# A mask and the norm's weights applied by column scalings on ScalarE in place of tensor operations on VectorE, with a new order of issue

## Chip, cores and metric

The kernel runs on one core of a Trainium2 chip. The core has five engines that run their own instruction streams and wait for each other by semaphores: TensorE (PE in the profile, PEld for its weight loads), VectorE (DVE), ScalarE (ACT), GpSimd (POOL) and SyncE (SP, which here only issues transfers). The metric is device microseconds of one launch. The kernel before took 1108.51 us, the median of three runs that lie between 1103.67 and 1111.27 us.

## What is computed

Two blocks follow each other. The first is a recurrence over 768 tokens for 4 batches of 8 heads with 40 channels each:

```
y[t]  = r[t] . state
Sa    = state . a[t]
state = state * w[t] - Sa (x) b[t] + v[t] (x) k[t]      # state is 40 x 40 per head
```

The second is a feed-forward block on the 3072 rows of 320 numbers that come out of the first:

```
x  = x / sqrt(mean(x*x) + 1e-6) * rms_g                 # rms_g: one weight per column
out = (silu(x @ w_gate) * (x @ w_val)) @ w_out          # 320 -> 1536 -> 320
```

All inputs are given as float64 or float32 and the products run in float32.

## The kernel before

The 768 tokens are cut into 24 chunks of C = 32 tokens; all 32 sequences (4 batches x 8 heads) of a chunk are worked on together. Each chunk has three stages:

- `front(c)` loads the chunk's tokens, turns them with TensorE, and builds the decayed keys and the products between tokens of the chunk, level by level (distances 1, 2, 4, 8, 16). Its result is a triangular matrix per sequence, in `LT`, which goes through DRAM (`sB`) into the layout `M`.
- `inverse(c)` inverts these triangles on VectorE: 31 steps, each a multiplication into `tmp` and a subtraction from `Yi` which depends on it and which the next step depends on. The result goes through DRAM (`sY`) back into `LT`.
- `main(c)` carries the state across the chunk and computes the outputs. Here the product `score` gives a 32 x 32 matrix per sequence in PSUM (`sc`). For each of the five levels a masked part of `sc` is written to `As` (192 instructions in all, lines 853 to 863), then five `level` products read `As`, and `y` gathers them. Afterwards `y` is turned (`turn4`), normalised into `x` by ScalarE, turned once more (`turn3`), and multiplied by the norm's weights `gcol` into `xg` (line 920), with the model's channels on the partitions.

Two chunks make a group. `feed(g)` runs the feed-forward block for a group: for each of 12 slices of the hidden width it makes two products of `xg` with a weight slice `wf` (gate and value), `Silu` of the gate on ScalarE into `sg`, the product of both on VectorE into `hT`, and the output product into `po`. For the first group the weights are also converted from float64 by integer operations on VectorE and ScalarE (`narrow`, tiles `wf`, `ex`, `o`), and kept in DRAM (`sW`).

PSUM is used as three pairs of banks (`ps0` to `ps2`) for everything but `po`. A product takes a pair and holds it until all that read it are issued. A pair is one tile; the framework that sets the semaphores also makes two engines that read the same bank wait for each other.

Nothing is scheduled while the kernel is built. Every operation is recorded as a piece (`Plan.add`), with what it depends on, and the pieces are then issued one by one in the order that the table `ORDER` gives, with the PSUM pair that the table `PAIRS` gives. A number in `ORDER` names the next piece, counted from the first one that is not issued yet, and a "-" issues a filler product of the identity (line 1000) which keeps TensorE active; there are 280 of them, all before the first output products. So the order of each engine's instructions is fixed by a table that the kernel only plays back, and each engine runs its own in that order.

All recorded operations of a kind have one line in the profile, that of the helper: 475 is every VectorE operation, 502 a copy on ScalarE, 498 an activation, 505 a scaling on ScalarE (`scale`), 518 a transfer, 521 a product, 524 a turn. So the profile is read by tiles.

Of the kernel before, what the change touches and what calls it, by code (L numbers as in the profile page):

```python
# [7 lines left out]
FP32 = mybir.dt.float32  # L8
# [8 lines left out]
P = 128  # L17
C = 32
LEVELS = (1, 2, 4, 8, 16)
CG = 2  # L20
WB = 5
S0, S1 = 15.0, 2.0
LEAD = 2
WARM = 230.0
# [21 lines left out]
36 33 2 26 42 1 31 0 25 343 37 29 107 38 24 36 26 34 262 2 13 1 35 40 0 190 24 339 13 14 - - - 40 17 44 15 41 43 55  # L46
42 8 60 47 175 72 48 45 84 185 59 68 186 585 54 58 - - - - - 49 93 586 53 179 69 71 599 81 176 57 597 50 67 178 609
70 188 80 622 51 92 16 623 65 610 52 56 177 633 64 66 - - - - - - - - - - - - 61 189 9 598 77 79 187 78 587 620 62 0
587 81 - - - - 72 75 179 82 62 90 595 384 194 588 87 11 633 89 589 74 395 620 197 590 380 88 73 195 391 - - - - 101
196 209 390 610 84 102 214 381 201 611 202 5 212 86 213 383 591 85 0 222 92 591 611 17 95 221 224 223 384 94 234 225  # L50
- - 197 233 237 93 391 245 246 592 328 393 198 598 645 612 0 641 598 15 612 592 - 338 205 206 380 642 599 209 0 207
612 200 0 337 612 186 598 6 326 613 2 599 641 34 176 200 216 217 23 600 389 215 33 201 355 95 202 177 96 214 - - - -
211 187 339 93 0 577 0 561 578 297 579 171 192 53 187 191 - - - 182 188 200 623 172 185 625 186 580 562 581 612 355
582 199 1065 197 583 611 183 198 624 184 0 152 1005 850 298 0 298 0 837 295 0 0 0 83 130 298 148 0 298 83 0 507 307
833 0 303 555 0 840 307 0 290 0 67 125 316 314 0 132 125 67 0 0 131 314 0 286 325 0 130 0 298 130 0 291 292 - - - -
- 287 0 293 0 304 0 316 305 301 0 0 283 0 296 0 311 0 322 281 0 286 0 295 280 0 292 - - - - - - - - - - - - - - - -
- 288 0 0 0 0 301 0 285 62 301 116 305 0 283 250 116 0 - - - - - - - - 293 0 258 112 296 0 110 300 256 0 308 307 245
293 292 0 0 304 0 288 0 301 - - - - - - 298 306 0 0 313 0 297 0 0 0 293 310 494 301 0 494 0 302 0 0 299 492 0 0 296
0 246 0 791 0 0 0 787 0 0 93 468 2 796 94 469 0 94 462 794 0 467 93 94 290 461 95 462 96 468 511 97 469 291 98 470
481 289 99 292 471 0 99 100 101 471 102 472 103 481 511 104 482 105 488 106 489 107 483 2 490 108 109 0 293 109 490  # L60
0 108 0 0 379 0 379 387 0 387 369 0 405 378 387 406 0 - - - - - - - - - - - - - - - - - - - - - - - - - - - - - - -
- - - - - - - - - - - - - - - - - - - - - - - - - - - - - - - - - - - - - - - - 44 0 367 377 0 415 0 42 0 414 383 43
412 0 383 410 0 383 40 373 0 0 0 0 0 0 36 0 377 - - - - - - - - - - - - - - - - - 44 0 377 35 44 0 414 0 0 82 0 32 -
43 0 373 0 90 0 229 407 38 88 0 40 78 226 42 38 41 47 48 0 43 226 42 50 45 48 396 0 50 396 43 0 396 0 0 379 395 380
0 395 380 0 401 0 394 0 378 242 400 44 0 400 47 0 145 45 377 242 0 145 391 377 0 216 1 145 391 42 635 398 429 626
146 0 397 39 145 426 634 398 146 147 631 43 623 44 621 45 632 46 148 47 622 - - - - 639 375 376 149 48 416 239 641
830 150 399 377 640 840 0 150 641 653 48 838 151 658 152 645 828 - - - - - - 642 153 670 154 646 155 682 49 656 50
156 669 657 51 157 666 158 667 52 159 643 668 - - - - - - - 53 389 160 161 678 162 1 651 652 - 647 2 702 655 3 654 0
594 610 611 609 625 595 636 109 608 110 596 373 - - - - - - - - - - - 605 590 374 111 345 783 607 626 782 383 112
627 620 622 385 793 113 623 606 375 382 114 792 621 - - - - - - - 617 384 115 376 346 116 377 619 117 635 634 118  # L70
618 378 119 - - - - - 160 633 120 379 121 163 380 161 122 381 123 162 124 164 386 - - - - - - - - - 629 125 387 126
127 128 388 129 630 130 640 631 389 638 131 390 - - - - - 167 641 132 391 133 639 134 392 168 135 393 - - - - - 165
136 394 137 138 430 139 166 571 431 581 643 140 - - - 171 721 644 580 141 642 142 570 143 174 645 144 173 145 178 -
- - 182 175 146 177 147 172 150 149 179 - - - 180 148 637 176 185 732 432 186 433 0 1065 584 283 - 39 1064 36 582 38
284 638 37 40 635 583 0 17 635 480 625 567 497 40 18 624 498 41 284 568 626 42 285 499 627 43 570 286 642 636 44 500
2 706 287 45 643 897 0 493 500 501 643 287 897 656 644 648 2 45 597 907 502 649 494 0 457 860 458 0 613 0 457 611
552 0 - 596 457 621 598 0 622 0 456 595 610 853 457 622 458 634 854 0 505 - - - 500 360 765 521 361 449 531 519 764
504 532 543 362 508 363 0 500 517 543 501 4 515 363 502 364 506 419 514 365 5 366 516 367 0 367 419 368 421 369 370
420 422 44 0 370 - 430 371 44 0 3 40 0 367 426 368 369 370 504 371 37 372 373 374 375 429 376 526 525 521 377 505
522 0 338 466 390 339 397 377 9 340 391 341 392 342 430 393 398 343 480 440 400 378 439 395 387 429 396 394 403 408  # L80
388 0 403 0 342 474 700 403 578 0 700 403 342 709 490 343 0 474 7 696 405 343 709 475 403 344 0 487 706 472 0 485
695 10 343 704 404 0 404 0 4 404 37 405 0 401 31 337 481 402 45 0 474 3 337 338 41 339 402 0 42 3 0 398 705 399 471
50 335 400 898 336 703 470 401 337 37 907 338 339 402 27 480 699 908 704 340 403 341 897 479 486 701 889 343 700 584
478 890 713 714 481 899 702 719 28 706 559 900 342 712 29 560 731 30 0 531 9 0 9 683 684 17 10 0 10 454 0 450 552 10
451 0 10 672 0 672 - - - - - - - - - - - - - - - - 662 25 0 27 670 26 0 682 680 24 695 539 677 676 678 704 661 37 -
- - - 3 36 675 662 296 4 681 434 691 663 679 692 703 672 5 0 0 428 1 680 683 42 682 666 43 687 681 667 20 40 686 21
677 695 2 22 292 0 675 705 287 0 675 287 688 0 671 0 669 665 269 7 17 410 8 682 29 411 412 30 667 413 414 0 8 665 0
675 8 681 672 9 674 0 9 672 - - - - - - - - - - 481 0 9 37 483 411 0 471 0 25 5 401 6 402 403 404 471 7 39 405 473 -
- - - - - - - - - - - 16 0 0 28 8 27 397 0 397 28 0 397 0 654 462 0 5 396 36 8 397 398 37 399 14 47 462 15 0 457 10
723 44 3 11 43 458 583 644 21 12 646 582 4 13 645 461 0 571 21 13 572 458 393 22 14 394 15 466 0 391 455 19 0 372 0  # L90
16 436 0 694 28 5 27 442 6 695 371 439 7 0 696 0 451 370 435 6 760 0 745 0 428 0 741 362 425 0 751 433 362 741 0 748
362 0 425 423 358 733 0 358 0 744 358 432 359 360 0 427 428 0 7 359 0 359 15 0 359 360 6 0 425 0 428 442 359 360 361
362 363 364 0 360 361 742 362 0 362 363 364 419 365 742 366 367 2 368 423 751 369 370 371 372 373 424 675 374 7 0
424 2 0 1154 672 0 1154 421 422 732 432 738 0 669 730 1002 732 670 420 995 731 439 742 685 985 421 0 993 421 687 735
422 686 743 4 1002 423 748 736 991 424 746 983 366 757 367 759 368 425 992 369 744 0 369 746 371 757 755 370 759 768
425 767 736 582 0 582 3 583 584 0 584 751 0 582 746 774 0 731 0 431 737 731 747 421 745 0 731 364 580 0 580 739 581
582 439 583 584 2 424 585 740 757 0 759 740 753 754 760 585 755 586 750 366 587 424 588 365 589 425 364 590 419 591
363 752 592 593 0 347 174 346 175 331 176 342 177 0 177 178 0 178 7 179 342 180 181 359 182 8 183 184 185 186 187
188 189 12 341 190 352 191 192 349 193 194 350 224 195 196 351 0 222 9 224 5 0 4 217 7 0 214 328 335 218 16 332 226
219 343 344 0 417 223 267 338 182 224 266 183 13 184 276 185 0 183 222 184 274 185 186 223 187 330 188 20 189 338 0  # L100
229 223 0 223 188 189 190 191 226 194 227 192 3 225 229 193 224 239 4 0 231 4 0 228 7 233 193 234 238 235 338 339
236 340 532 341 239 12 530 240 194 241 533 195 242 541 197 243 0 538 240 9 608 10 241 536 338 4 13 339 527 242 340
192 539 243 341 342 343 244 0 339 340 240 341 342 0 538 342 240 343 0 16 343 324 344 539 737 345 346 538 727 540 552
# [290 lines left out]
def kernel(  # L394
# [41 lines left out]
    N = 8  # L436
# [116 lines left out]
    for j, l in enumerate(LEVELS):  # L553
        nc.vector.tensor_scalar(iw[:, 2], iw[:, 0], j, None, ALU.logical_shift_right)
        nc.vector.tensor_scalar(msk[:, j], iw[:, 2], 1.0, None, ALU.is_equal)
# [477 lines left out]
```

## Time and profile before

| | before |
|---|---|
| median of three runs | 1108.51 us |
| profiled execution | 1109.57 us, of which 1107.8 us from first to last instruction |
| VectorE, in `As` | 192 instructions: 144 of 128x256 and 48 of 128x512, 83.2 us |
| VectorE, in `xg` | 24 instructions of 128x384, 13.5 us |
| ScalarE, all | 989 instructions |
| filler products | 560 matrix instructions, 72.9 us |

How to read it: "busy" is the time in which an engine executed an instruction, as a share of the span. TensorE's is taken from ends that are modelled, so busy is not the same as at its peak. In a line of instruction groups the form `out<-in` names the tiles written and read, then comes the shape as partitions x elements, the count, the total busy time, the mean of one in ns, and the idle time of the engine just before these instructions, with what ended it. In a table of stretches each engine's busy time in that stretch stands with its number of instructions, then PEclk, the clock granted to TensorE as a share of the full one, and the share of the transfer engines. In a list of waits the columns are total us, number of waits, and the longest.

### The profile page before, as it was taken

The page shows a single profiled execution, that of the slowest core. Times are in us where ns is not written, and L with a number is a line of the kernel's source. Part 1 is how long each engine was busy: PE and PEld are TensorE (multiplying, and loading weights), DVE is VectorE, ACT ScalarE, POOL GpSimd, SP SyncE. Part 2 cuts the span into 40 slices and gives each one's busy share as a digit, 9 for nine tenths or more (in the row PEclk, how much of TensorE's full clock was granted, in tenths as well). Part 3 has the DMA queues.
Part 4 walks back from the last instruction along what each step waited for, and adds up shares of the span by engine and source line. Part 5 has one row for each costly group of instructions (what it writes and reads, how often), then busy time and mean ns, then how long its engine had stood idle before and what let it go on. Part 6 is the DMA issues. An engine that isn't in the chain of part 4 may idle for free.

```text
span 1107.8 us, 53122 instructions
## 1 busy us (share of the span) xinstructions
PE 1043.1 (94%) x23152; PEld 862.2 (78%) x23152; DVE 906.1 (82%) x3065; ACT 453.9 (41%) x989; POOL 302.4 (27%) x534
## 2 busy tenths in 40 slices
PE   5698889989999999999999999999999999999998
PEld 5597777867878877877877887877878788888876
DVE  5999998899798889799789689988878889798421
ACT  4645554644235335325335335325325335332211
POOL 7621344022323422412422422422303412200000
PEclk9799999989999999999999999999979999999999
DMA  7635555675645645546535635635546536434242
GB/s 158 155 75 155 132 115 133 188 225 143 160 120 121 157 104 141 132 118 151 126 99 139 149 107 150 142 96 151 119 108 149 126 109 150 108 108 130 80 141 80
DMA packets 171177, 145.43 MB, mean 131 GB/s; under 512 B 123712, under 2 KB 142080, under 8 KB 170944
## 3 DMA queue, kind: packets, MB, share of 16 engines
q1 hardware_dynamic: 152576, 119.06, 39.7%
q0 software_dynamic: 16192, 22.64, 10.5%
q8 instruction: 182, 2.98, 1.2%
q10 hardware_dynamic: 2176, 0.33, 0.2%
q14 instruction: 51, 0.42, 0.1%
HBM read 125.83 MB, written 16.12 MB: 128 GB/s over the span
## 4 chain that ended last, share of the span: by engine, by line
PE 59%; DVE 26%; issue 4%; DMA 4%; ACT 4%; POOL 2%; SPq 1%; DVEq 0%; POOLq 0%; ACTq 0%
PE ps L521 40%; PE po L521 11%; PE ps L524 8%; DVE LT L475 4%; DVE tmp L475 3%; DVE Yi L475 3%; DVE K L475 2%; DVE As L475 2%; DVE ex L475 2%; DVE wf L475 2%; DVE y L475 1%; SPq L518 1%; DVE Ab L475 1%; ACT K L502 1%; DVE r L475 1%
## 5 line engine op out<-in xcount | busy, mean ns | idle before, releaser
L521 PE MATMUL ps<-xg,wf 128*128 128x256 f32 (+1 forms) x1728 | 357.6, 395 | 2.5 <-DVE xg L475 1.6
L521 PEld LDWEIGHTS ps<-xg,wf 128*128 128x128 f32 (+1 forms) x1728 | 263.1, 190 | 58.0 <-issue 15.2
L521 PE MATMUL po<-wf,hT 128*128 128x320 f32 x576 | 178.6, 444 | 2.7 <-DVE hT L475 1.3
L475 DVE TENSOR_TENSOR tmp<-Yi,M 128x60 f32<-128x60 f32 (+24 forms) x744 | 156.1, 210 | 19.2 <-DMA M<-sB 3.0
L475 DVE TENSOR_TENSOR Yi<-Yi,tmp 128x60 f32<-128x60 f32 (+24 forms) x744 | 155.4, 209 | 15.9
L498 ACT ACTIVATE sg<-ps 128x256 f32<-128x256 f32 x144 | 53.6, 382 | 239.9 <-PE ps L521 222.9
L518 POOL DMA_DIRECT2D VU<-in_v_dram x92 | 53.3, 586 | 354.0 <-PE ps L524 207.5
L521 PEld LDWEIGHTS po<-wf,hT 128*128 128x128 f32 x576 | 102.3, 190 | 38.8 <-issue 3.7
L475 DVE TENSOR_TENSOR hT<-ps,sg 128x256 f32<-128x256 f32 x144 | 59.3, 419 | 54.7 <-ACT sg L498 53.4
L521 PEld LDWEIGHTS ps<-Ab,K 40*64 40x64 f32 x4608 | 77.8, 139 | 30.5 <-issue 9.7
L475 DVE TENSOR_TENSOR K<-K,T 128x512 f32<-128x512 f32 (+1 forms) x192 | 93.5, 495 | 8.8 <-ACT K L502 3.0
L521 PE MATMUL ps<-Ab,K 40*64 40x56 f32 x4608 | 87.4, 226 | 11.2 <-DVE K L475 3.1
L502 ACT COPY K<-K 128x256 f32<-128x256 f32 (+1 forms) x168 | 71.3, 443 | 61.8 <-PE ps L521 38.5
L475 DVE TENSOR_TENSOR As<-ps,msi 128x256 f32<-128x256 f32 (+1 forms) x192 | 83.2, 481 | 13.1 <-PE ps L521 12.9
L502 ACT COPY KN<-ps 128x640 f32<-128x640 f32 x96 | 66.4, 692 | 54.8 <-PE ps L524 21.4
L521 PEld LDWEIGHTS ps<-As,KN 128*40 128x40 f32 x3072 | 67.2, 125 | 18.7 <-issue 10.7
L521 PE MATMUL ps<-As,KN 128*40 128x32 f32 x3072 | 74.5, 206 | 6.1 <-issue 3.4
L1000 PE MATMUL po<-ident 128*128 128x128 f32 x560 | 72.9, 284 | 5.3 <-ACT po L544 5.3
L518 POOL DMA_DIRECT2D kbn<-in_b_dram x92 | 53.8, 587 | 83.0 <-PE ps L521 72.3
L518 POOL DMA_DIRECT2D wn<-in_w_dram x92 | 51.5, 565 | 85.7 <-DVE tmp L475 32.5
L518 POOL DMA_DIRECT2D kbn<-in_k_dram x92 | 53.3, 583 | 75.0 <-PE ps L521 74.3
L1000 PEld LDWEIGHTS po<-ident 128*128 128x128 f32 x560 | 67.6, 197 | 6.7 <-POOL wan L514 5.2
(124 smaller groups left out, 1546.8 us busy)
## 6 DMA issues: line engine op xcount, KB each, us to landing
wf<-sW SPq DMA_DIRECT2D x144, 480.0 KB, 4.1
M<-sB SPq DMA_DIRECT2D x96, 128.0 KB, 3.7
rn<-in_r_dram SPq DMA_DIRECT2D x24, 160.0 KB, 4.3
sW<-ex SPq DMA_DIRECT2D x16, 240.0 KB, 3.0
out_dram<-o SPq DMA_DIRECT2D x48, 80.0 KB, 3.6
kbn<-in_b_dram POOLq DMA_DIRECT2D x92, 40.0 KB, 3.1
wan<-in_w_dram POOLq DMA_DIRECT2D x46, 80.0 KB, 4.2
wan<-in_a_dram POOLq DMA_DIRECT2D x46, 80.0 KB, 4.0
```

The costliest lines, as they stand in the source:

```text
L475: plan.add("DVE", time + more + each * size(o), 0.087, lambda at: fn(at(o), *m(at)), [o], aps(*args))
L498: scalar(o, [a], lambda at: nc.scalar.activation(at(o), at(a), f, **kw), aps(acc), 0.1 if f in (AF.Square, AF.Relu) else 0.0)
L502: scalar(o, [a], lambda at: nc.scalar.copy(at(o), at(a)), extra=more)
L518: plan.add(by, 0.6 if by == "POOL" else 0.45, 0.0, lambda at: queue.dma_start(out=o, in_=i), [o], [i], load=LOADS[load], since=since)
L521: return o, lhsT, rhs, lambda at: nc.tensor.matmul(at(o), lhsT, rhs, start=start, stop=stop, skip_group_check=True), 4
L524: return o, i, ident, lambda at: nc.tensor.transpose(at(o), i, ident), 2
L1000: plan.warm = lambda: nc.tensor.matmul(po_[:, 0, DM:DM + P], ident, ident, start=False, stop=False, skip_group_check=True)
```

## The change

Three things change in `main`, and the tables are new.

1. Of the five masks, the one of the last level (distance 16) has for each partition the same value in all of its 16 columns. The operation on VectorE that multiplied all 512 numbers per partition of both halves by the mask (`G == 1`) is replaced by two `scale` operations on ScalarE of 256 numbers each, which multiply by one mask value per partition. The other masks stay on VectorE.
2. The multiplication of the turned `x` by the norm's weights, one operation of 384 numbers on VectorE, is replaced by three `scale` operations on ScalarE of 128 numbers each, with one weight per partition.
3. `ORDER` and `PAIRS` are replaced by new tables: 6199 pieces instead of 6127, and 276 fillers instead of 280. The counts of pieces on TensorE (897), GpSimd (507) and SyncE (712) are the same; VectorE has 2995 instead of 3043 and ScalarE 1088 instead of 968.

Code for another way to invert the triangles is added too, under `c < BLOCKS` with `BLOCKS = 0`, so it is never built; what stays of it is one small constant, `lower`, made once at the start.

```diff
+BLOCKS = 0
 ...
 ORDER = """
-36 33 2 26 42 1 31 0 25 343 37 29 107 38 24 36 26 34 262 2 13 1 35 40 0 190 24 339 13 14 - - - 40 17 44 15 41 43 55
 ...
+    lower = const.tile([P, 1], FP32, name="lower")
+    nc.vector.tensor_scalar(lower, msk[:, 4, 0:1], -1.0, None, MUL)
 ...
         for j, l in reversed(list(enumerate(LEVELS))):
             G = C // (2 * l)
-            if G == 1 or l == 1:
-                tt(As[:, j], sc.rearrange("p o n t -> p (o n) t")[:, :, None, 1 if l == 1 else 16:C:2 if l == 1 else 1].to_broadcast((P, NI, 2, 16)),
+            if G == 1:
+                for i in range(2):
+                    scale(As[:, j, :, i], sc.rearrange("p o n t -> p (o n) t")[:, :, 16:C], msi[:, j, i, 0:1])
+            elif l == 1:
+                tt(As[:, j], sc.rearrange("p o n t -> p (o n) t")[:, :, None, 1:C:2].to_broadcast((P, NI, 2, 16)),
                    msi[:, j:j + 1].to_broadcast((P, NI, 2, 16)), MUL)
 ...
-        tt(xg[c // CG][:, :, c % CG * P:(c % CG + 1) * P], ps, gcol[:, :, None].to_broadcast((P, KT, P)), MUL)
+        for kt in range(KT):
+            scale(xg[c // CG][:, kt, c % CG * P:(c % CG + 1) * P], ps[:, kt], gcol[:, kt:kt + 1])
```

## The prediction, made before the result was known

> **What bounds the kernel now.** I read the page first, then stretches of the span, then single groups, then waits. From the page, the share of each engine and the granted clock in 40 slices:
>
> ```profile
> PE 1043.1 (94%) x23152; PEld 862.2 (78%) x23152; DVE 906.1 (82%) x3065; ACT 453.9 (41%) x989; POOL 302.4 (27%) x534
> PEclk9799999989999999999999999999979999999999
> ```
>
> The average hides two stages. The table of stretches parts them (busy us and instructions per engine, then clock, transfers):
>
> ```profile
> 27.00:177.00 150.00, 128.26 (x3003) 115.58 (x3001) 143.38 (x480) 78.75 (x155) 50.85 (x87) 0.93 0.50 124
> 177.00:267.00 90.00, 82.64 (x1686) 67.92 (x1686) 80.00 (x244) 48.75 (x97) 22.80 (x38) 0.96 0.69 190
> 267.00:360.00 93.00, 91.47 (x2008) 74.17 (x2007) 79.43 (x272) 37.89 (x89) 24.57 (x42) 1.00 0.51 129
> 360.00:1024.00 664.00, 647.45 (x15225) 529.64 (x15225) 567.54 (x1973) 263.29 (x593) 182.71 (x312) 0.99 0.51 128
> ```
>
> The third number is TensorE, the fifth VectorE. To 177 us VectorE is busy 143.4 of 150 us: it bounds, and TensorE's 128 us hold most of the 72.9 us of fillers. From 177 to 267 both are near 90%. From 267 on TensorE bounds: it idles 18.1 us of 757, VectorE 110. So a saving on VectorE is worth its length early, and almost nothing later.
>
> **What leaves VectorE.** By shape, the two groups concerned and two rows that price their replacement:
>
> ```profile
> L475 DVE TENSOR_TENSOR As<-ps,msi 128x512 f32<-128x512 f32 x48 | 32.3, 682 | 8.0 <-PE ps L521 8.0
> ...
> L475 DVE TENSOR_TENSOR xg<-ps,gcol 128x384 f32<-128x384 f32 x24 | 13.5, 562 | 5.2 <-PE ps L524 5.1
> L505 ACT ACTIVATE x<-ps,ss 128x320 f32<-128x320 f32 x24 | 12.7, 530 | 10.1 <-POOL ss L508 10.0
> ...
> L505 ACT ACTIVATE Xs<-ps 128x320 f32<-128x320 f32 x24 | 10.4, 435 | 16.4 <-PE ps L521 16.1
> ```
>
> Half of the 48 wide `As` are the mask of the last level. Per chunk 682 + 562 = 1244 ns go, 29.9 us in 24 chunks. That is the upper end. The lower one comes from how VectorE overlaps the ends of instructions, seen in its timeline:
>
> ```profile
> 326.94 0.20 DVE L475 TENSOR_TENSOR tmp<-Yi,M 128x48 f32<-128x48 f32 x1
> 327.05 0.41 DVE L475 TENSOR_TENSOR As<-ps,msi 128x256 f32<-128x256 f32 x1
> 327.39 0.20 DVE L475 TENSOR_TENSOR Yi<-Yi,tmp 128x48 f32<-128x48 f32 x1
> ```
>
> `Yi` needs `tmp`. With an `As` of 0.41 us between them it starts 0.45 us after `tmp`; elsewhere in the timeline, with nothing between, about 0.25. So a mask set between the steps of the inversion costs only 0.20 us, 0.21 below its duration. With the same rebate the wide one costs 0.47 and `xg` 0.35, together 0.82 per chunk. I take the middle, 1.03.
>
> Up to 267 us there are four wide pairs of `As` and four `xg` (first 99.7 and 146.4 us): 4.1 us, between 3.3 and 5.0. Two chunks lie in the bound stretch and count in full, two in the mixed one and count half: **-3.1 us**.
>
> **What comes to ScalarE.** `x` and `Xs` have the same shape and differ in the scale's source, a column or a constant: 95 ns. The 128x640 copy from PSUM takes 692 ns, `Xs` 435 for 320: 0.8 ns per element. So a 256 scaling with a column is 530 - 51 = 479 ns, a 128 one 530 - 154 = 376; per chunk 2 x 479 + 3 x 376 = 2.09 us, or 50 us in all, and ScalarE goes from 41 to 45%. That the trace has such activations (`x`) without table loads in the loop speaks against a cost of that kind.
>
> The Trainium skill's page "ScalarE: Activation LUTs", section "Rules for kernel authors", speaks against the change: multiplications belong on VectorE. In engine time the rows agree, 2.09 us in place of 1.24, and by that rule the sum would be 20 us for the worse; by the trace only what reaches the bounding engine counts.
>
> **The new wait.** Both engines now read one `sc` pair, and readers of one pair are kept apart. This is seen already, beside the wait that ScalarE mostly has:
>
> ```profile
> ACT sg L498 <- PE ps L521: 222.9, 97, 7.6
> ...
> ACT KN L502 <- DVE LT L475: 9.9, 12, 2.1
> ```
>
> `KN` and `LT` read the same product on two engines, and wait in turn. In the new order the two scalings stand in the midst of VectorE's seven masks of the chunk in most chunks, so VectorE must pause between two masks for 0.96 us and two handoffs, unless it has other work there. I counted it: mostly three to six steps of the inversion (0.23 us each) or a `K` product stand in the gap, and cover it; in chunks 15 and 21 one operation stands there, leaving some 0.6 us, in five others 0.2. Sum 2.2 us; of the first four chunks 0.7 us: **+0.7 us**. Bounds: 0, and 4 x 1.1 = 4.4 us if the cover fails everywhere early; queued behind it are then `tmp`, `Yi` and the weights' conversion. The Trainium skill's page "PSUM — Partial Sum Buffer", section "PSUM bank collisions raise a hardware error", says why such readers must be kept apart; leaving the wait out is no option by it.
>
> **After 267 us.** TensorE's waits there that end with VectorE's tiles sum to 6.4 us, with ScalarE's to 4.4; its weight loads' to 22.2 and 23.0. VectorE is busy 668 us there, ScalarE 315. Taking 20 x 1.24 = 25 us from the one and adding 20 x 2.09 = 42 to the other, in proportion: VectorE -0.2 (matmuls) to -0.8 (loads), ScalarE +0.6 to +3.1. Middle: -0.5 and +1.8: **+1.3 us**. At the end one `xg` stands alone on the path:
>
> ```profile
> 1061.72 4.12 PE L521 MATMUL ps<-xg,wf 64*128 64x256 f32 x24 [0.65 <-DVE xg L475]
> ```
>
> In the new order too the last `turn3` is followed at once by products that need the last `xg`; three scalings (1.13 us, about 0.95 with the 0.1 by which two copies of `K` overlap) take the place of 0.57: **+0.4 us**. `lower` is one VectorE operation at the start, where the nearest, `msk`, take 0.18: **+0.2 us**.
>
> **The order.** Transfers are the same in number on SyncE and GpSimd; queues are permuted, not longer. Among TensorE's 897 pieces each `front`, `main` and `feed` begins at most 7 places from where it did, mostly within 1. Unknown is what the permutation does to the clock. In the TensorE-bound stage the clock was halved once:
>
> ```profile
> 810.00:813.00 3.00, 1.39 (x65) 1.03 (x65) 2.84 (x7) 0.10 (x1) 0.00 (x0) 1.00 0.52 150
> 813.00:816.00 3.00, 2.45 (x125) 2.37 (x128) 2.56 (x7) 1.56 (x4) 0.00 (x0) 0.65 0.07 20
> 816.00:819.00 3.00, 3.00 (x55) 2.57 (x52) 2.47 (x8) 1.72 (x3) 0.46 (x1) 0.50 0.02 5
> ```
>
> After 2.2 us of idling within 6, clocks of 0.65, 0.50, 0.50, 0.50, 0.57 over 15 us: 6.8 us of clock lost. The new order may lose this spell or gain one: -6.8 to +6.8. I take 0, as nothing in the order tells which.
>
> **Sum.** -3.1 + 0.7 + 1.3 + 0.4 + 0.2 = -0.5 us: 1109.1 against the profiled 1109.57. That execution lies 1.1 us above the median of the runs, 1108.51, so I forecast **1108 us**, no change to be told. One per cent (11 us) is about what a measurement of this kernel can tell from none, as its three runs spread over 7.6 us.
>
> **Rivals.**
>
> 1. *The cover is better than counted and the half-clock spell goes*: -5.0 early, -6.8 for the clock, with the shorter hold on the `sc` pair (VectorE's masks of a chunk shrink from 3.85 to 3.17 us) taking a tenth of TensorE's 18 us of idling, -1.8: **1095 us**. For it: VectorE's 95.6%. Against: nothing says that the spell hangs on `As` or `xg`; an `LT` ended the idling. Chance 0.16.
> 2. *ScalarE becomes late* (the other side). Its queue is strict in order: `Silu` of a hidden slice stands behind 0.96 or 1.13 us of scalings that wait for `sc` or `turn3`. Behind `Silu` wait `hT`, the output product and the PSUM pair, so TensorE. Of the 42 us added after 267, one third on TensorE's path is +14: **1122 us**; it decides over 1% from 11.5 of the 42 on. Against: ScalarE waited 222.9 us for products before `Silu`; it is early. Chance 0.14.
> 3. *The change doesn't free VectorE*: the handoffs cost as much as the masks gave, cover failing throughout. Early +4.4 in place of +0.7: **1112 us**. Chance 0.14, within 1%.
> 4. *One more half-clock spell*: **1115 us**, chance 0.08, within 1%; two would be slower than that.
>
> My forecast has 0.48. Faster by over 1%: 0.16; within: 0.68 (0.48, most of rivals 3 and 4); slower: 0.16 (rival 2 and two spells). The range reaches from near rival 1 to near rival 2, 1097 to 1120.
>
> **What would show it.** VectorE's busy time down by 25 to 32 us and ScalarE's up by 43 to 52; 48 scalings `As<-ps,msi` of 450 to 500 ns and 72 `xg` of 350 to 400; waits of VectorE's `As` for ScalarE of 1 to 5 us in all; TensorE's idling after 267 us again 15 to 25 us; the last `xg` 0.9 to 1.2 us before the last feed. It is wrong if `Silu`'s start moves behind scalings, if half-clock spells differ in the TensorE-bound stage, or if the early stage ends more than 5 us sooner or later.

## The result and the profile after

The changed kernel is a little slower. Over runs that alternate with those of the kernel before its median is 1113.65 us (18 runs, 1109.73 to 1123.76) against 1111.30 us (18 runs, 1103.67 to 1120.56) of the kernel before; the ratio is 1.0042, with a 95% interval of 1.0017 to 1.0067. That is 4.7 us by the ratio (1.9 to 7.4 by the interval), inside the forecast range and within one per cent, but on the other side of no change than the forecast sum of -0.5 us, and clear of no change.

The profiled execution took 1117.87 us, 8.3 us more than that of before. This single execution lies 4 us above its median, so a difference of a few us between the two traces isn't read as the change's. From its page, the share of each engine, and the queue that brings TensorE's instructions (packets, MB, share of the transfer engines):

```profile
PE 1048.2 (94%) x23144; PEld 862.5 (77%) x23144; DVE 884.4 (79%) x3018; ACT 490.5 (44%) x1109; POOL 301.7 (27%) x534
...
q8 instruction: 182, 2.98, 1.1%
```

VectorE lost 21.7 us of busy time and ScalarE gained 36.6. Busy time counts stretches in which two instructions overlap once, so these sums are smaller than the durations. The table of stretches of the kernel after (third number TensorE, fifth VectorE, sixth ScalarE):

```profile
27.00:177.00 150.00, 132.29 (x3075) 120.50 (x3067) 141.22 (x475) 83.53 (x172) 47.95 (x83) 0.95 0.50 123
177.00:267.00 90.00, 79.39 (x1616) 63.35 (x1612) 79.28 (x240) 50.60 (x104) 24.36 (x41) 0.91 0.70 189
267.00:360.00 93.00, 89.97 (x1942) 72.40 (x1943) 75.13 (x264) 39.35 (x94) 24.56 (x42) 0.98 0.50 129
360.00:1024.00 664.00, 644.40 (x15220) 524.17 (x15217) 551.64 (x1942) 288.97 (x676) 182.28 (x312) 0.99 0.51 127
```

VectorE has come down from 85.5 to 82.8% in the last two stretches together (647.0 and 626.8 us busy of 757) and TensorE idles 22.6 us there where it idled 18.1. The moved operations, by shape (busy time, then the mean of one in ns):

```profile
L508 ACT ACTIVATE xg<-ps,gcol 128x128 f32<-128x128 f32 x72 | 22.3, 369 | 11.0 <-PE ps L527 10.7
L508 ACT ACTIVATE As<-ps,msi 128x256 f32<-128x256 f32 x48 | 20.6, 471 | 41.3 <-DVE As L478 32.5 <-PE ps L524 5.4 <-DVE tmp L478 3.1
L478 DVE TENSOR_TENSOR As<-ps,msi 128x512 f32<-128x512 f32 x24 | 16.4, 684 | 1.1 <-PE ps L524 1.1
```

The chain between the two engines, from the list of waits of the kernel after (total us, number, longest):

```profile
DVE hT L478 <- ACT sg L501: 68.0, 45, 7.8
...
ACT As L508 <- DVE As L478: 32.5, 17, 4.9
...
DVE As L478 <- ACT As L508: 2.2, 3, 1.5
```

VectorE waits 2.2 us for the scalings; ScalarE waits 32.5 us for VectorE's masks before its own. The first line was 53.4 us before the change: VectorE now waits more for `Silu`. Last, what TensorE waits for between 267 and 1060 us. After:

```profile
PE ps L524 <- issue: 12.2, 17, 1.8
PE ps L524 <- DVE LT L478: 1.5, 3, 0.7
...
PE ps L524 <- ACT xg L508: 0.9, 2, 0.6
```

and before:

```profile
PE ps L521 <- issue: 4.3, 10, 0.9
PE ps L521 <- DVE LT L475: 2.2, 3, 1.4
```

All the additional idling of TensorE is in the row "issue": it waits for no engine that the profile knows. Added up over all rows from 267 us to the end, its waits that end with VectorE fell from 7.1 to 5.3 us, those that end with ScalarE stayed at 4.4, and "issue" rose from 5.6 to 13.0. The next section is about this row as much as about the moved operations.

### The profile page after: what moved, and what is told of

Read it like the earlier page. It is cut to its first block, busy times and chain, and to the rows that moved or that the text cites. A ratio compares the mean times of both kernels' runs of the same rounds, so it can differ in the third digit from the quotient of the medians.

```text
span 1116.1 us, 53179 instructions
## 1 busy us (share of the span) xinstructions
PE 1048.2 (94%) x23144; PEld 862.5 (77%) x23144; DVE 884.4 (79%) x3018; ACT 490.5 (44%) x1109; POOL 301.7 (27%) x534
## 4 chain that ended last, share of the span: by engine, by line
PE 69%; DVE 19%; issue 4%; ACT 3%; DMA 2%; POOL 1%; SPq 0%; DVEq 0%; ACTq 0%; POOLq 0%
PE ps L524 46%; PE po L524 14%; PE ps L527 8%; DVE Yi L478 2%; DVE tmp L478 2%; DVE LT L478 2%; PE po L1037 2%; DVE ex L478 2%; DVE As L478 2%; DVE y L478 2%; DVE wf L478 1%; DVE K L478 1%; DVE Ab L478 1%; DMA sY<-Yi 1%; DVE r L478 1%
## 5 line engine op out<-in xcount | busy, mean ns | idle before, releaser
L524 PE MATMUL po<-wf,hT 128*128 128x320 f32 x576 | 182.7, 450 | 1.5 <-DVE hT L478 1.2
L521 POOL DMA_DIRECT2D VU<-in_v_dram x92 | 53.4, 586 | 360.4 <-PE ps L527 210.2
L501 ACT ACTIVATE sg<-ps 128x256 f32<-128x256 f32 x144 | 53.4, 384 | 173.3 <-PE ps L524 165.6
L524 PEld LDWEIGHTS ps<-Ab,K 40*64 40x64 f32 x4608 | 75.5, 134 | 30.4 <-issue 13.2
L505 ACT COPY KN<-ps 128x640 f32<-128x640 f32 x96 | 66.3, 691 | 51.2 <-PE ps L527 19.8
L1037 PE MATMUL po<-ident 128*128 128x128 f32 x552 | 78.3, 299 | 5.3 <-ACT po L547 5.3
L478 DVE TENSOR_TENSOR As<-ps,msi 128x256 f32<-128x256 f32 (+1 forms) x168 | 68.2, 455 | 17.7 <-PE ps L524 14.7
L524 PEld LDWEIGHTS ps<-As,KN 128*40 128x40 f32 x3072 | 65.4, 124 | 16.4 <-issue 10.1
L1037 PEld LDWEIGHTS po<-ident 128*128 128x128 f32 x552 | 72.6, 211 | 6.6 <-POOL wan L517 5.2
L521 POOL DMA_DIRECT2D kbn<-in_k_dram x92 | 53.2, 583 | 89.2 <-PE ps L524 88.4
L521 POOL DMA_DIRECT2D wn<-in_w_dram x92 | 51.5, 565 | 89.4 <-DVE KN L478 32.3
L524 PE MATMUL ps<-As,KN 128*40 128x32 f32 x3072 | 72.1, 204 | 3.0 <-DVE As L478 1.5
L521 POOL DMA_DIRECT2D kbn<-in_b_dram x92 | 53.4, 585 | 66.6 <-PE ps L524 58.6
```

The costliest lines, as they stand in the source:

```text
L478: plan.add("DVE", time + more + each * size(o), 0.087, lambda at: fn(at(o), *m(at)), [o], aps(*args))
L501: scalar(o, [a], lambda at: nc.scalar.activation(at(o), at(a), f, **kw), aps(acc), 0.1 if f in (AF.Square, AF.Relu) else 0.0)
L505: scalar(o, [a], lambda at: nc.scalar.copy(at(o), at(a)), extra=more)
L521: plan.add(by, 0.6 if by == "POOL" else 0.45, 0.0, lambda at: queue.dma_start(out=o, in_=i), [o], [i], load=LOADS[load], since=since)
L524: return o, lhsT, rhs, lambda at: nc.tensor.matmul(at(o), lhsT, rhs, start=start, stop=stop, skip_group_check=True), 4
L1037: plan.warm = lambda: nc.tensor.matmul(po_[:, 0, DM:DM + P], ident, ident, start=False, stop=False, skip_group_check=True)
```

## What the row "issue" is

One of these stops in the timeline of the kernel after (start, length, instructions, idle time before in brackets):

```profile
402.67 0.68 PE L524 MATMUL ps<-Ab,K 40*64 40x56 f32 x29
404.36 0.73 PE L524 MATMUL ps<-Ab,K 40*64 40x56 f32 x34 [1.01 <-issue]
```

TensorE stops for 1.01 us in the midst of a group of products that were all released together. I counted TensorE's instructions in the trace from the first one (products, weight loads and the few that carry only a semaphore) and took the place modulo 256. Of the stops of 0.3 us or more within a group of products after 267 us, the kernel after has 14, together 11.2 us, and each of them lies at place 193 or 194. The kernel before has 7, together 3.0 us, six of them at these places. The period is that of the instruction queue shown above: its 182 packets of 16.4 KB stand against 46,288 products and loads, 254 for each packet. So each packet is a block of 256 instructions; in the example the transfer of a packet ran from 402.04 to 403.00 us, and TensorE went on 1.36 us after it landed.

The kept traces show that the fetching of a block is what TensorE waits for. In each of the 14 stops of the kernel after, TensorE goes on between 1.22 and 1.55 us after the packet with the block's own number has landed, while the stops themselves last from 0.34 to 1.79 us. At the 144 block places after 267 us, with or without a stop, it never goes on sooner than 1.22 us after that landing. In all 18 traces the soonest is 1.11 us, and the stops at these places end 1.11 to 1.73 us after the landing. What happens when the blocks are moved was tested (below).

A stop can cost more than its own length. The longest one came with a spell of 6.83 us at half the clock, seen here in TensorE's timeline and in the stretch from 896 to 899 us (the granted clock is 0.50):

```profile
896.05 0.47 PE L524 MATMUL ps<-Xs,LT 32*32 32x40 f32 x11 [1.79 <-issue]
...
896.00:899.00 3.00, 2.95 (x16) 2.08 (x16) 1.55 (x5) 1.73 (x4) 0.00 (x0) 0.50 0.02 5
```

In the five traces of kernels with the new order and without moved blocks there are nine half-clock spells between 267 us and the last 10 us. Each begins during a stop of 0.9 to 1.8 us at a block place, or within 2 us of its end.

The Trainium skill's page "Runtime: NRT & Kernel Launch", section "Instruction fetch mechanics", has the same blocks of 16 KiB, 256 instructions, and says that crossing their boundary is mostly hidden. In the kernel before it mostly is: 3.0 us of stops. The runs below show it unhidden with up to 31 us.

## The experiments

All ratios are to the kernel before in the same series of runs. Four kernels at first take the two parts of the change apart, the operations and the tables. Where a kernel has the old operation in the new order, it stands at the place of the first of the scalings; where it has the scalings in the old order, they stand one after the other at the place of the old operation. A table can be rewritten in this way for both, because pieces keep their relative order.

**The old operations in the new order.**

```diff
 ORDER = """          # the new table, with the old pieces
-            if G == 1:
-                for i in range(2):
-                    scale(As[:, j, :, i], ...)
+            if G == 1 or l == 1:
+                tt(As[:, j], ...)
-        for kt in range(KT):
-            scale(xg[...][:, kt, ...], ps[:, kt], gcol[:, kt:kt + 1])
+        tt(xg[...], ps, gcol[:, :, None].to_broadcast((P, KT, P)), MUL)
```

> The kernel before with the new order and PSUM pairs: the last level's mask and the norm's weights are VectorE operations as before, each standing where the first of the scalings stood. Theory 'order': the new sequence itself is what costs, so this is about 0.4% slower than the kernel before, like the changed kernel. Theory 'engine': the move to ScalarE costs (scalings that stand in ScalarE's queue ahead of Silu; pauses between VectorE's masks), so this is within 0.15% of the kernel before, or up to 0.3% slower if the new order only suits the shorter VectorE work.

Measured: 1120.30 us, ratio 1.0110 (1.0076 to 1.0145). With the old operations the new order costs 12 us (8 to 16), which the prediction took as 0. It is more than either theory had, 0.4% or at most 0.3%. Its list of TensorE's waits from 267 to 1060 us has the longer row again:

```profile
PE ps L521 <- issue: 8.5, 12, 1.8
```

**The new operations in the old order, both and each alone.**

```diff
 ORDER = """          # the old table, with the new pieces
-            if G == 1 or l == 1:                  # new_ops_old_order, as_old_order
-                tt(As[:, j], ...)
+            if G == 1:
+                for i in range(2):
+                    scale(As[:, j, :, i], ...)
-        tt(xg[...], ...)                          # new_ops_old_order, xg_old_order
+        for kt in range(KT):
+            scale(xg[...][:, kt, ...], ps[:, kt], gcol[:, kt:kt + 1])
```

> The changed operations in the old order: two scalings stand where the wide mask stood, three where the product with the weights stood. Theory 'order': within 0.15% of the kernel before, faster if anything, since VectorE has 25 us less to do. Theory 'engine': at least 0.4% slower. In the old order VectorE's next mask follows the two scalings at once in most chunks, so the pause of about 1 us per chunk has no cover: VectorE's waits for As on ScalarE should sum to 10 to 20 us, against 2.2 in the changed kernel; if that pause decides, the time is 0.5 to 1% above.

> The mask alone goes to ScalarE, in the old order. Theory 'pause between the masks': it carries all of the loss that the kernel with both changes in the old order has, 0.3 to 1%. Theory 'late Silu': half of the loss or less, since 0.95 of the 2.1 us per chunk that ScalarE gains are here.

> The norm's weights alone go to ScalarE, in the old order. Theory 'pause between the masks': no loss, 0 to 0.4% faster, since VectorE is relieved of 0.55 us per chunk and nothing of it waits in turn. Theory 'late Silu': 0.2 to 0.5% slower, the waits of hT for Silu rise from 20 to 25 us or more.

Measured: both moves 1117.87 us, ratio 1.0086 (1.0058 to 1.0115); `As` alone 1112.86 us, 1.0041 (1.0019 to 1.0063); `xg` alone 1110.67 us, 1.0019 (0.9997 to 1.0042). In the order of before, the two moves cost 9.5 us; for `xg` alone the interval includes no change, and `As` alone carries about half of the loss, so neither theory is borne out in full. Two waits of the kernel with both moves, VectorE's in the whole run and TensorE's from 267 to 1060 us, say where a part of it goes:

```profile
DVE As L478 <- ACT As L508: 21.9, 21, 4.0
```

```profile
PE ps L524 <- ACT xg L508: 4.0, 9, 1.0
PE ps L524 <- issue: 3.9, 7, 0.9
```

Here VectorE pauses 21.9 us for the scalings of `As`, more than the 16.4 us (24 x 682 ns) that it was relieved of, and in the changed kernel, whose order puts other work of VectorE into the pauses, it was 2.2 us. The stops of TensorE are as few as before the change. The half-clock spell at 814 us of the kernel before is absent in both traces of the old order with `As` moved, and is there at 818 us with `xg` moved alone: the two with `As` moved are slower although they lack a spell that takes 6.8 us of clock.

**Each move alone in the new order**, with the edits above taken one at a time:

```diff
-            if G == 1:                            # xg_new_order keeps the old As
+            if G == 1 or l == 1:
-        for kt in range(KT):                      # as_new_order keeps the old xg
+        tt(xg[...], ...)
```

> The new order with only the mask on ScalarE; the norm's weights are one VectorE operation at the place of the first scaling. Both moves together take the new order from 1.0110 to 1.0042 of the kernel before. If both carry alike this lies near 1.007; if the mask alone carries it, near 1.004; if the mask's pauses cost, above 1.011.

> The new order with only the norm's weights on ScalarE; the mask is one wide VectorE operation at the place of the first scaling. Near 1.007 if both carry alike, near 1.004 if the weights alone carry the gain, 1.011 or more if the mask alone does.

Measured: `As` alone 1120.61 us, 1.0070 (1.0047 to 1.0094); `xg` alone 1118.16 us, 1.0061 (1.0035 to 1.0087). Together the four corners are below. They come from different series, partly on different chips, each as a ratio to the kernel before in its own series.

| | old order | new order |
|---|---|---|
| old operations | 1 | 1.0110 |
| `As` moved | 1.0041 | 1.0070 |
| `xg` moved | 1.0019 | 1.0061 |
| both moved | 1.0086 | 1.0042 |
| stops within groups after 267 us, one trace each | 1.4 to 4.6 us | 7.9 to 11.2 us |

The new order is worse than the old by 1.1% with the old operations, and better by 0.44% with the new ones (1.0042 / 1.0086 = 0.9956; from the two intervals about 0.992 to 0.999). In the new order the two moves gain 0.67% (1.0042 / 1.0110 = 0.9933, about 0.989 to 0.998), and one alone 0.4 or 0.5% (1.0070 and 1.0061 against 1.0110, each uncertain by about 0.4%, so that a gain by one alone is hardly clear of none). So the move is worth 7.5 us where the order makes room for it, and costs 9.5 us where it doesn't.

**Moving the code blocks.** A filler consists of two products and two loads. In three kernels 16, 32 or 48 fillers of one long run of them, all before the first output products, are replaced by products of half the width, twice as many; so all later instructions of TensorE stand 64, 128 or 192 places further in their blocks of 256, a quarter, half and three quarters. The same with 32 is done to the kernel before.

```diff
-- - - - - - - - ...
+= = = = = = = = ...                               # 16, 32 or 48 of them
+            if word == "=":
+                self.order.append(None)
+                self.half(), self.half()
+                continue
+    plan.half = lambda: nc.tensor.matmul(po_[0:64, 0, DM:DM + 64], ident[:, 0:64], ident[:, 0:64], start=False, stop=False, skip_group_check=True)
```

> The changed kernel; 16 of the 75 fillers in the long run before the first state products are each split into two of half the columns and rows, so that 64 instructions are added on TensorE in about the same time, and all later ones stand a quarter of a 256-instruction block further on. In the changed kernel TensorE stops for 11.2 us after 267 us inside groups of products where no wait stands, each time on the first instruction of a block of 256, about 1 us after a transfer of the instruction queue; in the kernel before for 3.0 us. Theory 'code loading': these stops move to other places, their sum changes by several us (anything from 1 to 12), and the time follows it nearly one to one. Theory 'order': stops and time stay as in the changed kernel, within 0.15%.

> As above with 32 fillers split: half a block further on. Theory 'code loading': the stops sum to another value than 11.2 us after 267 us; over the four shifts of the changed kernel time and stops rise and fall together, and the best shift is at least 0.4% faster than the changed kernel, near the kernel before or below it. Theory 'order': all four shifts lie within 0.3% of each other.

> As above with 48 fillers split: three quarters of a block further on. Same expectations.

> The kernel before, 32 of its fillers split: half a block further on. Theory 'code loading': the 3.0 us of stops after 267 us are a lucky place; half a block on they are more, 4 to 10 us, and the kernel is 0.2 to 0.6% slower than without. Theory 'order': no change beyond 0.15%.

Measured, as ratios to the kernel before: after with 16 1.0325 (1.0303 to 1.0347), with 32 1.0409 (1.0376 to 1.0442), with 48 1.0265 (1.0226 to 1.0303); before with 32 1.0464 (1.0421 to 1.0507), which is 1160.58 us. So the places among the blocks matter in both orders, and both kernels stand at favourable ones: against the same kernel without the shift, half a block costs 3.7% in the new order (1.0409 / 1.0042) and 4.6% in the old. The expectations had the direction for the kernel before, not the size (0.2 to 0.6%), and that the best shift of the changed kernel would gain, which none did. The waits of TensorE from 267 to 1108 us, of after with 32 (12.2 us without the shift) and of before with 32 (4.3 us without):

```profile
PE ps L528 <- issue: 33.0, 27, 3.4
```

```profile
PE ps L525 <- issue: 30.6, 25, 2.9
```

The stops within groups are 25.6, 30.8 and 21.3 us in the three kernels, and 30.3 us in before with 32, with all but one at places 193 and 194 of the shifted count. They are not all of the loss: TensorE's granted clock in the stretch from 360 to 1024 us is 0.97 in the kernel with 32, against 0.99. The stops and the half-clock spells after 267 us (half of a spell's length is lost) account together for most of the loss, single traces against those of the same kernel without the shift:

| | stops, us more | clock lost, us more | profiled time, us more |
|---|---|---|---|
| after with 16 | 14.3 | 8.5 | 26.8 |
| after with 32 | 19.6 | 22.2 | 44.4 |
| after with 48 | 10.0 | 8.5 | 24.7 |
| before with 32 | 27.3 | 17.1 | 49.7 |

The cut fillers themselves are not what costs: the last scaling into `x` of chunk 3, at 258 us, ends at most 6.2 us later than in the kernel without the shift, and the rest of the loss comes after it.

**Two fillers less**, which moves everything behind them 8 places back.

```diff
-- - - - - ... (two of them)
```

> The changed kernel with two of the 75 fillers of the long run left out, so that all that follows on TensorE stands 8 instructions earlier against the blocks of 256; the fillers left out took 0.4 us where TensorE waits. Theory 'code loading': a shift of 8 of 256 moves the block boundaries within groups of 128 instructions; TensorE's stops change, by several us if the new tables were made for their place among the blocks: 0.3 to 2% slower. Rival: a place among the blocks is matched only roughly, and a shift of 8 changes nothing beyond 0.2%.

Measured: 1117.36 us, ratio 1.0041 (1.0016 to 1.0066), the same as the kernel after. The stops stay:

```profile
PE ps L524 <- issue: 9.7, 14, 1.8
```

The expected loss of 0.3 to 2% didn't come. This one small shift changes nothing; a version of the new order without its extra stops was not found.

**What a microsecond of VectorE or ScalarE is worth.** The sum of the prediction rests on such prices. Each of these kernels has the order and operations of before and issues some operations several times, with the same result each time.

```diff
+        plan.add("DVE", ..., lambda at: [fn(at(o), *m(at)) for _ in range(times)], ...)
-                   msi[:, j:j + 1].to_broadcast((P, NI, 2, 16)), MUL)
+                   msi[...], MUL, times=7 if G == 1 and c < 4 else 1)         # before_dve_early
+                   msi[...], MUL, times=7 if G == 1 and 12 <= c < 16 else 1)  # before_dve_late
+        copy(Y, eye, times=8 if c >= 6 else 1)                                 # before_act_late
+                copy(side(K1[:, :, x], l, 1), side(K[:, :, x], l, 1), times=2 if c >= 6 else 1)      # before_act_grains
+                    tt(side(K1[:, :, x], l, 0), ..., MUL, times=2 if c >= 6 else 1)                  # before_dve_grains
```

> The kernel before; the wide mask of the last level is written seven times instead of once in chunks 0 to 3, the same values into the same place. That adds 24 x 0.61 to 0.68 us = 14.6 to 16.4 us of VectorE work before 267 us. The prediction's first term counts VectorE's time there in full for chunks 0 and 1 and half for 2 and 3: +11 to +12 us, 1.0%. Rival: VectorE's time is not what sets the early stage's end (transfers, code loading or the clock do): less than +5 us.

> As above in chunks 12 to 15, where TensorE bounds. By the prediction VectorE's time is worth almost nothing there: +0 to +4 us, although it comes in four lumps of 4 us. Rival: VectorE's masks lie on the path there too (the pair of banks is held, the level products wait): +10 us or more.

> The kernel before; the copy of the unit matrix at the head of each inversion is made eight times from chunk 6 on, the same values into the same place. That adds 18 x 7 x 0.31 to 0.40 us = 39 to 50 us of ScalarE work after 267 us, about what the change adds (42), in lumps of 2.2 to 2.8 us, and nothing else. The prediction's term (+1.8 us, 0.6 to 3.1) says 0 to 0.3%. Rival 2 (late Silu) says a third of it, +13 us or 1.2%.

> The kernel before; from chunk 6 on each of the six copies of halves of K in a chunk is made twice on ScalarE (the same values). That adds 108 x 0.31 to 0.40 us = 33 to 43 us to ScalarE after 267 us, as the lumps did, but in grains of one copy. Theory 'lumps': grains are covered, +0 to +4 us. Theory 'every us counts': half of it as with the lumps, +17 to +21 us.

> The kernel before; from chunk 6 on each of the products of K with the decay at distances 4 and 8, four in a chunk... 72 in all of 0.43 us and 36 more at distance 16's neighbours where the loop makes them, is made twice on VectorE (for the first of two writes the same values are written). That adds 25 to 39 us to VectorE after 267 us, about what the change takes away (25). Theory 'lumps': covered, +0 to +5 us, so that taking 25 us away is worth nothing either. Theory 'every us counts': +25 us or more.

(The last one has 72 additional instructions, four in each of 18 chunks; the count given in its expectation is garbled.) The busy time that was added is the difference of the page's first line to that of before:

| added to | where | busy us more | ratio | us more by medians | us for each us |
|---|---|---|---|---|---|
| VectorE, lumps of six | chunks 0 to 3 | 17.7 | 1.0156 (1.0126 to 1.0187) | 17.0 | 1.0 |
| VectorE, lumps of six | chunks 12 to 15 | 18.2 | 1.0216 (1.0189 to 1.0242) | 24.7 | 1.4 |
| VectorE, single | chunks 6 to 23 | 28.9 | 1.0207 (1.0172 to 1.0241) | 24.4 | 0.8 |
| ScalarE, lumps of seven | chunks 6 to 23 | 48.7 | 1.0202 (1.0166 to 1.0238) | 21.3 | 0.4 |
| ScalarE, single | chunks 6 to 23 | 41.9 | 1.0059 (1.0033 to 1.0084) | 5.9 | 0.14 |

Early, each of the four chunks is late by 3.5 to 5 us more than the one ahead of it, about the lump's full length: against before, the first mask (at 99.7 us) starts 1.8 us later, and the scalings into `x` of chunks 0 to 3 end 6.2, 11.3, 16.3 and 19.8 us later. Late, a lump of VectorE reaches TensorE as a wait of the same size, here from 267 to 1060 us:

```profile
PE ps L521 <- DVE As L475: 12.4, 3, 4.3
...
PE ps L521 <- DVE Yi L475: 4.4, 3, 3.8
```

and half-clock spells follow it. Spread out as single instructions of 0.4 us it is nearly as dear, though no wait of TensorE for VectorE is long (TensorE's longest row from 267 to 1060 us):

```profile
PE ps L521 <- DVE LT L475: 5.6, 8, 1.9
```

But there are many of them: from 267 us to the end, TensorE's waits that end with VectorE sum to 24.4 us, against 7.1 before, and 5.1 us more of clock are lost. Together that is 22.4 of the 24.4 us. VectorE's share of the span stays at 82%, as the span grows with its work: 18% of idle time gave little cover. ScalarE's single copies, more than the change adds to its busy time, cost a seventh of their length.

These are prices of time added in the old order. No run takes time from VectorE without giving some to ScalarE, so that a microsecond saved is worth as much isn't shown.

## Why the prediction was wrong, by its steps

- *What leaves and what comes.* Right in size. The scalings of `As` take 474 ns at the median, 479 was worked out; those of `xg` 369 against 376; the busy times moved by less than forecast (-21.7 against -25 to -32, +36.6 against +43 to +52), as overlapping parts count once.
- *The new wait.* Right: 2.2 us in all, as counted. What the order is for shows in the old one, where the same two scalings hold VectorE 21.9 us.
- *The last `xg`.* Right that it is small: TensorE waits 0.72 us for it where it waited 0.65 (+0.1, +0.4 was forecast).
- *Early, two chunks full and two half.* The full price is right and the halves are not: time added to VectorE in the chunks 2 and 3 counts as fully as in 0 and 1. If time saved there counts alike, the term would be about -1 us more.
- *"So a saving on VectorE is worth its length early, and almost nothing later."* For time added, the second half is wrong: late microseconds on VectorE cost 0.8 us each when they come singly and 1.4 in lumps. I priced 25 us of late work in proportion to TensorE's waits, at -0.2 to -0.8 us; but the waits don't go in proportion, 28.9 us more on VectorE raised those that end with it from 7.1 to 24.4 us. For time saved it isn't settled. In single traces the two moves in the new order took these waits from 10.1 to 5.3 us, 4.8 us where the middle of the prediction had 0.5; against before they fell by 1.8 us. ScalarE's term (+1.8 us) doesn't show there: TensorE's waits that end with it went from 4.1 to 4.4 us. By the price of single copies, 0.14, the 49 us that both moves add in the whole run by their durations (48 x 0.471 + 72 x 0.369) would be about +7 us.
- *The order: "I take 0, as nothing in the order tells which."* This is the step that failed and turned the sign. With the old operations the new order costs 12 us. I compared the places of stages among TensorE's pieces, and looked for half-clock spells; the term stood at 0 without a measurement behind it. The places among the blocks of 256 instructions of TensorE's code were not looked at, although the row `PE ps L521 <- issue` led TensorE's waits already in the trace of before. In all five traces of the new order (with the two fillers less) the stops after 267 us are 7.8 to 11.2 us, in four of the old (before, and the three with moved operations) 1.4 to 4.6. How the miss is shared out depends on the way taken: by the order first it is +12 us for the order and -7.5 for the moves, by the moves first +9.5 for the moves and -4.9 for the order. The prediction counted its waits in the new order, so the first way is its own; there the terms of the moves, -0.5 us in sum, were off as well, on the other side.
- *The rivals.* None came. Rival 1's half-clock spell did go (the one at 814 us), and others came in its place, at 329 and 896 us, of 3.4 and 6.8 us length. The prediction held against it that nothing ties the spell to `As`; by the traces it goes when `As` is moved in the old order, and it is absent in all five of the new, with `As` moved or not. Rival 2's mechanism shows only with lumps: 49 us in lumps of seven cost 21 us, and TensorE's waits for `hT` are its longest row after 267 us (5.0 us); 42 us singly cost 6. In the changed kernel VectorE waits 14.6 us more for `Silu`, but TensorE's waits for VectorE didn't grow. Rival 3's handoffs don't come in the new order (2.2 us) and do come in the old one. Rival 4's 1115 us lies near the measured 1113.65 by luck: there is one spell more after 267 us, but less clock is lost in sum, 5.1 against 6.8 us.

So the sum is: the new order +1.1% with the old operations, the move in it -0.67%, together +0.42%. What in the new order costs the 1.1% isn't settled. The additional stops, some 5 us in the trace with the old operations (7.9 against 3.0), and the spell of 6.83 us at its stop of 1.80 us (at 897 us), 3.4 us of clock, make 8 of the 12 us; but the spell at 814 us, 6.8 us of clock, is gone in that trace, so most of the 12 us has no cause here. The old operation of VectorE, set where the new order has ScalarE's, may be a part. Since the new order also has these stops with the new operations, where it beats the old order by 0.44%, it may well be better still without them; whether and by how much is not known, as no shift tried took them away. No kernel run here beat the kernel before.

The prices don't add up to the moves in the old order. For `As` an estimate by them comes near: 20.8 us of pauses less 16.4 us of work, times 0.8, is +3.5 us, and 22.8 us of ScalarE times 0.14 +3.2 us, 6.7 us together; measured were 4.4. (The 20.8 us are VectorE's wait for these scalings in that kernel from 27 to 1060 us.) That is no confirmation, as the estimate leaves out the spell at 814 us, which that trace lacks. For `xg` they fail: 13.5 us off VectorE at 0.8 and 26.6 us on ScalarE at 0.14 give -7 us, and +2.2 were measured (-0.3 to +4.7); three scalings in turn stand between the turn and the products that need them, and TensorE's wait for `xg` rose from 0.9 to 4.0 us, which isn't enough for the 9 us. That stays open.

The Trainium skill's page "ScalarE: Activation LUTs", section "Rules for kernel authors", whose rule speaks against the change, would by the estimate that the prediction made from it have had 20 us for the worse. The runs give it its sign in the old order (+9.5 us) and not in the new one (-7.5 us).

## What to carry to other kernels

An order that was found for one set of operations isn't neutral for another: when a change brings both, run all four combinations, since here each of the two alone is a loss of about one per cent and together they cost 0.4. Price an engine's time by adding some, singly and in lumps, and not in proportion to its share in the waits of the bounding engine; and don't take the price of time added for that of time saved, which here failed for `xg`. And where the bounding engine stops in the midst of a group that waits for nothing, count its instructions to the next 256: one that is added or dropped upstream moves all that follows.

## What the runs showed of the hardware that was not expected

- TensorE's stops of 0.3 to 3.4 us at a fixed place of every 256 instructions, in streams of small products (40x56 and the like). They end 1.1 to 1.7 us after the block's packet has landed. A shift of all later code by 64 to 192 instructions cost 2.2 to 4.6%, in a kernel whose instructions otherwise are the same but for some fillers cut in two.
- A lump of six masks on VectorE late in the kernel costs more than its length (1.4 for each us): TensorE's waits that end with VectorE rose by 16.8 us from 267 us on, and half-clock spells took 8.5 us more of clock. In the clock records of the traces these spells last whole multiples of 3.41 us, from 3.4 to 23.9 us. After 267 us one of 3.4 us followed a stop of 1.06 us.
- Kernels whose instructions are the same up to the first mask at 100 us start it 1.5 to 3.5 us later than the kernel before in single traces. Differences of that size between two profiles are no evidence.
